# Staggering the first batch of an attention and FFN kernel: loads, weight conversion, norms and evictions moved between steps, and denominators by products with ones

## The chip, the core and the metric

The kernel runs on one core of one Trainium2 chip. The metric is the device time of one execution in microseconds (us); below it is the median of the runs shown. Profiles are of one execution each, taken by the hardware profiler. TensorE is written PE (its weight loads PEld), VectorE DVE, ScalarE ACT, GpSimd POOL, SyncE SP.

## What is computed

Attention over 8 batches, 12 heads, 448 positions, head dimension 64, with RMS norms of q and k, and then an FFN with a squared ReLU on 3584 tokens:

```
q_n, k_n = rmsnorm(q, g_q), rmsnorm(k, g_k)      # x / sqrt(mean(x*x) + 1e-6) * g
scores = matmul(q_n, k_n.T) / sqrt(64)
attn = exp(scores - max)
attn = attn / (sum(attn) + 1e-09)
x = matmul(attn, v)                              # (B,H,S,D) -> (B*S, H*D) = (3584, 768)
h = maximum(x @ w_in, 0.0)                       # w_in 768 x 2048
out = (h * h) @ w_out                            # w_out 2048 x 768
```

q, k, v are float32. The two weights reach the kernel as 64-bit floats, so it turns them into float32 itself.

## The kernel before

A flag computed from the gains chooses between two programs; the runs here take the one without the shift by the maximum (`shift=False`). Its work goes by pairs of heads: six pairs per batch, 48 in all (0 to 47), and four steps (`n` = 0 to 3) per pair, one for each quarter of the keys. Within a step the instructions are written out in an order that the engines keep (`manual_schedule`): every engine, and SP's DMA queue, works through its own instructions in program order and waits at each for what it needs.

For pair `i`:

- `load_qk` (L112) and `load_v` (L126) are DMAs on SP, into two buffers each.
- `normalize` (L135): per q and k, ACT squares, DVE reduces (L142), both times through the one buffer `squares`; DVE scales (L143), POOL raises to the power -1/2 (`rr`, L147; 112 x 16 numbers) and multiplies q by it (`qn`, L152). k's factor goes into the exponential's scale.
- `turn` (L165): eight transposes on PE into banks 2 and 3 (L173), DVE evicts qT with the gain (L175), ACT evicts kT (L179).
- `weigh` (L186), step `m`: PE's scores of both heads (L195) into banks 0 and 1 or, in odd steps, 2 and 3; ACT's exponentials (L197); `add_up` (L202) sums the weights of the steps, one head on POOL, one on DVE (L211).
- `attend` (L236), one pair later: PE multiplies weights and v (L244), accumulating over the four steps; in step 1 the summed weights are multiplied by ones (L251), which gives the denominators on the right partitions; DVE takes the reciprocal (L261), and after step 3 the product `xT` (L265).

A step of pair `i` issues `weigh(i, n)` and `attend(i - 1, n)`; step 0 also `normalize(i + 1)`, step 2 `turn(i + 1)`, step 3 `load_v(i + 1)`.

The FFN of batch b runs as a stream of pieces during batch b + 1, from its second pair on, so that the first pair of each batch has no FFN beside it. `ffn` (L279) first makes the 16 hidden tiles (L287, ACT's ReLU L296, squares on POOL L301 to L306) through banks 6 and 7, then the output tiles (L316), and stores them.

The weights stay in SBUF. They come in 56 chunks, 24 of w_in (128 x 512) and 32 of w_out (128 x 384). One chunk's conversion (`to_float32`, L365) is three ACT operations (L374 to L376) on the high and low words, a clamp on POOL (L377), and three DVE operations that join them (L382, L386, L390). The raw words of w_in lie in eight buffers (shared with `h2`), those of w_out in two (shared with `y`). `load_weights` (L352) issues a chunk's DMA and its conversion together, at the beginning of a step: one chunk per step in batch 0, three per step from pair 6 on.

The lines that the change and the prediction speak of are in these functions:

Of the kernel before, what the change touches and what calls it, by code (L numbers as in the profile page):

```python
# [10 lines left out]
F32 = mybir.dt.float32  # L11
# [22 lines left out]
def kernel(  # L34
# [33 lines left out]
    with tc.If(flag > 0) as either:  # L68
        program(tc, q, k, v, g_q, g_k, moe_w_in, moe_w_out, out, shift=False)
    with either.Else():  # L70
        program(tc, q, k, v, g_q, g_k, moe_w_in, moe_w_out, out, shift=True)
# [3 lines left out]
def program(ctx, tc, q, k, v, g_q, g_k, moe_w_in, moe_w_out, out, shift):  # L75
# [21 lines left out]
    gg = const.tile([P, 2], F32, name="gg")  # L97
# [12 lines left out]
    loaded, values, normal, turned, weights, sums, dens, xts = {}, {}, {}, {}, {}, {}, {}, {}  # L110
# [23 lines left out]

    def normalize(i):  # L135
# [10 lines left out]
        rr = small.tile([CP, 2, 2 * NJ], F32, name="rr", tag="rr", bufs=3)  # L146
# [89 lines left out]
    def attend(i, m):  # L236

        b, c = pairs[i]
        vt = values[i]
        if m == 0 and c == 0:  # L240
            xts[b] = [None] * NC
        av = banks[4 + i % 2][:, 0:S]
        for e in range(2):
            nc.tensor.matmul(  # L244
                av[ds(e * D, D), :], lhsT=vt[:, e, m, :], rhs=weights.pop((i, e, m)),
                start=m == 0, stop=m == NJ - 1,
            )
        if m == 1:
            den = banks[5 - i % 2][:, 0:S]
            for e in range(2):  # L250
# [12 lines left out]
        if m == NJ - 1:  # L263
            xT = ffn_p.tile([P, S], F32, name="xT", tag="xT", bufs=NC + 2)
            nc.vector.tensor_tensor(out=xT, in0=av, in1=dens.pop(i), op=ALU.mult)  # L265
            xts[b][c] = xT
            del turned[i], normal[i], values[i]
# [74 lines left out]
    def weight_chunks():  # L342
# [5 lines left out]
        for f in range(NF):  # L348
            for half in range(2):
                yield w_out_sb[:, f, ts(half, HALF)], moe_w_out[ts(f, P), :], half * HALF  # L350

    def load_weights(dst, rows, col):  # L352
        n = dst.shape[1]
        if rows.dtype == F32:
# [4 lines left out]
        words = ffn_p.tile([P, n, 2], U32, name="words", tag=tag, bufs=bufs)  # L359
        nc.sync.dma_start(  # L360
            words.rearrange("p n w -> p (n w)"), rows.bitcast(U32)[:, 2 * col : 2 * (col + n)]
        )
        to_float32(dst, words[:, :, 0], words[:, :, 1])

    def to_float32(dst, low, high):  # L365
# [15 lines left out]
        bits = dst.bitcast(U32)  # L381
# [9 lines left out]

    load_qk(0)
    for e in range(2):
        for n, gain in enumerate((g_q, g_k)):
            nc.scalar.dma_start(gg[ds(e * D, D), n : n + 1], gain.rearrange("(d one) -> d one", one=1))
    nc.vector.scalar_tensor_tensor(
        out=g, in0=gg[:, 0:1], scalar=D**-0.5, in1=gg[:, 1:2], op0=ALU.mult, op1=ALU.mult
    )
    nc.vector.memset(minus_half, -0.5)
    nc.vector.memset(ones, 1.0)  # L400
    make_identity(nc, ident)
    load_qk(1)
    load_v(0)
# [4 lines left out]
    chunks = deque(weight_chunks())  # L408

    with tc.manual_schedule(engines=ENGINES):  # L410
        normalize(0)
        turn(0)
        stream, pieces, done = iter(()), 0, 0
        for i, (b, c) in enumerate(pairs):
            if i + 2 < len(pairs):
                load_qk(i + 2)
            for n in range(NJ):
                step = c * NJ + n
                if step == NJ and b:
                    stream, pieces, done = ffn(b - 1), ffn_pieces(b - 1), 0  # L420
                for _ in range(1 if b == 0 else len(chunks) if shift else 3):
                    if chunks:
                        load_weights(*chunks.popleft())
# [3 lines left out]
                if shift and n == 0 and i:  # L427
                    for m in range(NJ):
                        attend(i - 1, m)
                weigh(i, n)  # L430
                if i and not shift:
                    attend(i - 1, n)
                if n == 0 and i + 1 < len(pairs):
                    normalize(i + 1)
                if n == 2 and i + 1 < len(pairs):
                    turn(i + 1)
                if n == NJ - 1 and i + 1 < len(pairs):
                    load_v(i + 1)
            if c == NPAIR - 1:
                for _ in stream:  # L440
                    pass
        for n in range(NJ):
            attend(len(pairs) - 1, n)
# [32 lines left out]
```

## Time and profile before

| | us |
|---|---|
| median of 3 runs (1873.43 to 1875.64) | 1874.79 |
| the profiled execution, its own time | 1875.46 |
| its span in the trace | 1873.4 |
| PE busy (share of the span) | 1675.4 (89%) |
| PE weight loads | 784.3 (42%) |
| DVE, ACT, POOL busy | 533.8, 473.6, 551.7 |
| mean granted clock of PE | 0.934 |

Busy time is the time an engine had an instruction in work; a matmul of float32 shows as several records (passes). The granted clock is given as a share of 2.4 GHz: 1.00, or 0.50 for 1.2 GHz, and values between are means over both. Times in rows are us from the start of the span; a bracket at the end of a row tells how long the engine sat idle before it, and what it waited for last.

### The profile page before, as it was taken

How to read it: one execution, taken by the hardware profiler on the slowest of the kernel's cores; microseconds unless marked ns; L12 is line 12 of the kernel's file. 1: busy time of each engine (PE TensorE's matmuls, PEld its weight loads, DVE VectorE, ACT ScalarE, POOL GpSimd, SP SyncE). 2: the span in 40 equal slices, each digit the busy share in tenths (PEclk: the TensorE clock that was granted, in tenths of full speed). 3: DMA queues.
4: the chain of work that ended last, by engine and by line, in shares of the span. 5: the costliest groups of instructions: out<-in, count | busy, mean ns of one | idle time of the engine just before them, and what ended most of it. 6: DMA issues, size and time to landing. Idle time of an engine off the chain costs nothing.

```text
span 1873.4 us, 14405 instructions
## 1 busy us (share of the span) xinstructions
PE 1675.4 (89%) x5440; PEld 784.3 (42%) x5440; DVE 533.8 (28%) x634; ACT 473.6 (25%) x853; POOL 551.7 (29%) x558
## 2 busy tenths in 40 slices
PE   3454367999999999999999999999999999999998
PEld 1111123454445544454445544454445534454555
DVE  3555555323212132223122222223222232212000
ACT  3435355312221122212221122212221132211100
POOL 3424233422332124313332224313341133311200
PEclk7665579999999999999999999999999999999999
DMA  4132243011010110011100110011000110000000
GB/s 139 60 105 74 82 116 108 23 32 38 22 24 24 32 38 15 16 38 32 30 15 24 32 38 15 20 42 38 15 15 24 32 38 15 20 22 9 0 9 27
DMA packets 80531, 70.24 MB, mean 37 GB/s; under 512 B 48196, under 2 KB 69700, under 8 KB 80452
## 3 DMA queue, kind: packets, MB, share of 16 engines
q1 hardware_dynamic: 80128, 69.23, 13.2%
q8 instruction: 45, 0.74, 0.2%
q14 instruction: 34, 0.28, 0.1%
q10 hardware_dynamic: 324, 0.00, 0.0%
HBM read 58.20 MB, written 11.01 MB: 37 GB/s over the span
## 4 chain that ended last, share of the span: by engine, by line
PE 80%; issue 5%; DVE 4%; POOL 4%; DMA 3%; ACT 2%; SPq 1%; POOLq 0%; ACTq 0%; DVEq 0%
PE bank L316 31%; PE bank L287 30%; PE bank L195 8%; PE bank L244 7%; POOL rr L147 2%; DMA words<-in_moe_w_out_dram 2%; PE bank L173 2%; PE bank L251 1%; DMA words<-in_moe_w_in_dram 1%; DVE rden L261 1%; POOL words L377 1%; DVE sum L211 1%; ACT words L374 1%; DVE w_in_sb L386 1%; DVE w_in_sb L382 1%
## 5 line engine op out<-in xcount | busy, mean ns | idle before, releaser
L287 PE MATMUL bank<-xT,w_in_sb 128*128 128x448 f32 x1536 | 612.1, 554 | 22.0 <-ACT h L296 20.7
L316 PE MATMUL bank<-w_out_sb,h 128*128 128x384 f32 x1792 | 593.9, 489 | 0.0
L316 PEld LDWEIGHTS bank<-w_out_sb,h 128*128 128x128 f32 x1792 | 335.5, 190 | 253.9 <-issue 32.2
L287 PEld LDWEIGHTS bank<-xT,w_in_sb 128*128 128x128 f32 x1536 | 291.4, 194 | 335.3 <-issue 287.6
L197 ACT ACTIVATE wT<-bank,rr 112x448 f32<-112x448 f32 x384 | 221.9, 629 | 553.9 <-PE bank L195 549.4
L195 PE MATMUL bank<-qT,kT 64*112 64x448 f32 x768 | 219.3, 638 | 101.2 <-DVE qT L175 70.6
L211 POOL TENSOR_TENSOR sum<-sum,wT 112x448 f32<-112x448 f32 x96 | 111.9, 1165 | 410.8 <-ACT wT L197 410.0
L211 DVE TENSOR_TENSOR sum<-sum,wT 112x448 f32<-112x448 f32 x96 | 109.8, 1143 | 421.3 <-ACT wT L197 421.3
L147 POOL TENSOR_TENSOR rr<-ms,minus_half 112x16 f32<-112x16 f32 x48 | 139.5, 2905 | 302.8 <-DVE ms L143 302.8
L244 PE MATMUL bank<-wT,vt 112*64 112x448 f32 x768 | 200.8, 605 | 0.0
L296 ACT ACTIVATE h<-bank 128x448 f32<-128x448 f32 x128 | 69.2, 542 | 424.1 <-PE bank L287 424.1
L195 PEld LDWEIGHTS bank<-qT,kT 64*112 64x112 f32 x768 | 61.8, 186 | 223.1 <-issue 101.4
L142 DVE TENSOR_REDUCE ms<-squares 112x8 f32<-112x512 f32 x96 | 65.8, 686 | 298.1 <-ACT squares L141 297.6
L261 DVE RECIPROCAL rden<-bank 128x448 f32<-128x448 f32 x48 | 141.5, 2948 | 1.2 <-PE bank L251 1.2
L306 POOL TENSOR_TENSOR h<-h 128x448 f32<-128x448 f32 x64 | 59.7, 932 | 183.3 <-ACT h L296 183.3
L211 DVE TENSOR_TENSOR sum<-wT 112x448 f32<-112x448 f32 x48 | 35.2, 734 | 228.6 <-PE bank L251 227.5
L244 PEld LDWEIGHTS bank<-wT,vt 112*64 112x64 f32 x768 | 40.4, 142 | 140.7 <-issue 140.7
L301 POOL TENSOR_TENSOR h<-h 128x384 f32<-128x384 f32 x64 | 53.3, 832 | 147.0 <-ACT h L296 147.0
L211 POOL TENSOR_TENSOR sum<-wT 112x448 f32<-112x448 f32 x48 | 71.0, 1479 | 75.9 <-PE bank L251 74.9
L173 PE MATMUL bank<-ident,qn 112*128 112x112 f32 x192 | 32.5, 298 | 67.8 <-POOL qn L152 51.3
L323 DVE COPY y<-bank 128x384 f32<-128x384 f32 x28 | 15.3, 548 | 229.8 <-PE bank L316 229.8
L141 ACT ACTIVATE squares<-qk 112x512 f32<-112x512 f32 x96 | 60.3, 628 | 39.8 <-DVE ms L142 39.7
(36 smaller groups left out, 580.7 us busy)
## 6 DMA issues: line engine op xcount, KB each, us to landing
words<-in_moe_w_in_dram SPq DMA_DIRECT2D x24, 512.0 KB, 6.6
words<-in_moe_w_out_dram SPq DMA_DIRECT2D x32, 384.0 KB, 3.1
qk<-in_q_dram SPq DMA_DIRECT2D x48, 224.0 KB, 3.3
qk<-in_k_dram SPq DMA_DIRECT2D x96, 112.0 KB, 3.5
vt<-in_v_dram SPq DMA_DIRECT2D x48, 224.0 KB, 2.9
out_dram<-y SPq DMA_DIRECT2D x8, 336.0 KB, 2.8
out_dram<-y SPq DMA_DIRECT2D x8, 288.0 KB, 2.7
out_dram<-y SPq DMA_DIRECT2D x8, 240.0 KB, 2.6
```

Source lines behind the costliest of these rows:

```text
L141: nc.scalar.activation(squares, qk[:, x], AF.Square)
L142: nc.vector.tensor_reduce(out=ms[:, ts(x, 2 * NJ)], in_=squares, axis=AX.X, op=ALU.add)
L147: nc.gpsimd.tensor_tensor(out=rr.rearrange("p x r -> p (x r)"), in0=ms, in1=minus_half.to_broadcast([CP, 4 * NJ]), op=ALU.pow,)
L173: nc.tensor.transpose(tr[:, ts(j, CP)], rows[:, j].rearrange("p h d -> p (h d)"), ident[:CP, :CP])
L195: nc.tensor.matmul(sc, lhsT=kT[r, ts(m, CP)], rhs=qT[r, :], start=True, stop=True)
L197: nc.scalar.activation(weights[i, e, m], sc, AF.Exp, scale=normal[i][2][:, 2 * m + e : 2 * m + e + 1])
L211: engine.tensor_tensor(out=sums[i, e], in0=so_far, in1=weights[i, e, m], op=ALU.add)
L244: nc.tensor.matmul(av[ds(e * D, D), :], lhsT=vt[:, e, m, :], rhs=weights.pop((i, e, m)), start=m == 0, stop=m == NJ - 1,)
L261: nc.vector.reciprocal(out=rden, in_=den)
L287: nc.tensor.matmul(ps, lhsT=w_in_sb[:, c, ts(f, P)], rhs=xT[c], start=c == 0, stop=c == NC - 1,)
L296: nc.scalar.activation(h[:, at : at + S], ps, AF.Relu)
L316: nc.tensor.matmul(ps, lhsT=h2[f][:, ts(n, P)], rhs=w_out_sb[:, f, ts(half, HALF)], start=f == 0, stop=f == NF - 1,)
```

## The change

Conversion of a chunk is cut in three and spread over steps: `load_weights(k)` issues only the DMA, `split_words(k)` the ACT and POOL part, `join_words(k)` the DVE part, one chunk behind. They are called at the end of a step, and w_in's chunks are loaded three ahead. For w_in, the last of ACT's three operations goes to POOL. w_out's chunks come by halves of the columns. One chunk per step is now taken through pair 6, three per step after it.

The squares of pair i + 2 are taken in step 3 of pair i, into two buffers. The eviction `xT` becomes `finish`, called in step 0 of the next pair but one. `load_v(i)` and `load_qk(i + 2)` stand behind it in step 0 of pair i.

In batch 0 (`alone`), the weights aren't summed: each step's weights are multiplied by ones, accumulating over four steps in bank 6 or 7, and the reciprocal follows step 3. The gain column `g` comes from a small matmul on the row that the flag was computed from; its own four DMAs go.

```diff
-    loaded, values, normal, turned, weights, sums, dens, xts = {}, {}, {}, {}, {}, {}, {}, {}
+    loaded, values, squared, normal, turned, weights, sums, dens, xts = {}, {}, {}, {}, {}, {}, {}, {}, {}
...
+    def square(i):
+        squares = [
+            att.tile([CP, 2 * NJ, D], F32, name="squares", tag="squares") for _ in range(2)
+        ]
+        for x in range(2):
+            nc.scalar.activation(squares[x], loaded[i][:, x], AF.Square)
+        squared[i] = squares
+
     def normalize(i):
...
-        for x in range(2):
-            squares = att.tile([CP, 2 * NJ, D], F32, name="squares", tag="squares", bufs=1)
-            nc.scalar.activation(squares, qk[:, x], AF.Square)
+        for x, squares in enumerate(squared.pop(i)):
             nc.vector.tensor_reduce(out=ms[:, ts(x, 2 * NJ)], in_=squares, axis=AX.X, op=ALU.add)
...
     def add_up(i, m):
 
-        if m == 0:
+        if m == 0 or pairs[i][0] == 0:
             return
...
     def attend(i, m):
...
+        alone = b == 0
         av = banks[4 + i % 2][:, 0:S]
+        den = banks[6 + i % 2 if alone else 5 - i % 2][:, 0:S]
...
+        for e in range(2):
+            wT = weights.pop((i, e, m))
+            if alone:
+                nc.tensor.matmul(
+                    den[ds(e * D, D), :], lhsT=ones, rhs=wT, start=m == 0, stop=m == NJ - 1
+                )
+            elif m == 1:
                 nc.tensor.matmul(
                     den[ds(e * D, D), :], lhsT=ones, rhs=sums.pop((i, e)), start=True, stop=True
                 )
+        if m == (NJ - 1 if alone else 1):
...
-        if m == NJ - 1:
-            xT = ffn_p.tile([P, S], F32, name="xT", tag="xT", bufs=NC + 2)
-            nc.vector.tensor_tensor(out=xT, in0=av, in1=dens.pop(i), op=ALU.mult)
...
+    def finish(i):
...
+        xT = ffn_p.tile([P, S], F32, name="xT", tag="xT", bufs=NC + 2)
+        nc.vector.tensor_tensor(
+            out=xT, in0=banks[4 + i % 2][:, 0:S], in1=dens.pop(i), op=ALU.mult
+        )
...
+    def split_words(k):
...
         nc.scalar.activation(high.bitcast(F32), high.bitcast(F32), AF.Copy, scale=REBIAS)
-        nc.scalar.activation(low.bitcast(F32), low, AF.Copy, scale=2.0**-29, bias=2.0**23)
-        nc.scalar.activation(low, low.bitcast(F32), AF.Copy, bias=-(2.0**23))
         nc.gpsimd.tensor_scalar(
             out=high.bitcast(F32), in0=high.bitcast(F32), scalar1=MOST, scalar2=-MOST,
             op0=ALU.min, op1=ALU.max,
         )
+        nc.scalar.activation(low.bitcast(F32), low, AF.Copy, scale=2.0**-29, bias=2.0**23)
+        if k < 4 * NC:
+            nc.gpsimd.tensor_scalar(
+                out=low, in0=low.bitcast(F32), scalar1=-(2.0**23), scalar2=1.0,
+                op0=ALU.add, op1=ALU.mult,
+            )
+        else:
+            nc.scalar.activation(low, low.bitcast(F32), AF.Copy, bias=-(2.0**23))
...
+    def convert(k):
+
+        join_words(k - 1)
+        if k + 3 < 4 * NC:
+            load_weights(k + 3)
+        elif k + 1 >= 4 * NC:
+            load_weights(k + 1)
+        split_words(k)
+
     load_qk(0)
+    load_weights(0)
+    load_qk(1)
+    load_weights(1)
+    load_weights(2)
...
         for i, (b, c) in enumerate(pairs):
...
             for n in range(NJ):
                 step = c * NJ + n
+                if n == 0:
+                    if i > 1 and not shift:
+                        finish(i - 2)
+                    load_v(i)
+                    if i + 2 <= last:
+                        load_qk(i + 2)
...
-                for _ in range(1 if b == 0 else len(chunks) if shift else 3):
-                    if chunks:
-                        load_weights(*chunks.popleft())
...
+                if i < last:
+                    if n == 0:
+                        normalize(i + 1)
+                    if n == 2:
+                        turn(i + 1)
+                    if n == NJ - 1 and i + 2 <= last:
+                        square(i + 2)
+                for _ in range(1 if i < NPAIR + 1 else 3):
+                    if piece <= len(chunks):
+                        convert(piece)
+                        piece += 1
```

## Rows read from the trace of the kernel before

**Rows 1.** The span in 40 slices, granted clock of PE in tenths

```profile
PEclk7665579999999999999999999999999999999999
```

**Rows 2.** Windows: from:to, length, busy time per engine (instructions), PE clock, DMA share, GB/s

```profile
97.30:128.80 31.50, 15.13 (x46) 4.66 (x46) 17.22 (x22) 13.12 (x23) 10.82 (x9) 0.61 0.27 89
...
193.10:245.50 52.40, 18.42 (x52) 5.57 (x52) 27.46 (x44) 22.31 (x44) 13.08 (x16) 0.57 0.34 99
...
245.50:338.00 92.50, 70.53 (x205) 30.44 (x204) 52.73 (x82) 48.17 (x95) 40.65 (x51) 0.88 0.36 103
338.00:456.90 118.90, 118.90 (x402) 57.64 (x401) 28.45 (x32) 24.41 (x44) 29.75 (x28) 1.00 0.09 25
```

**Rows 3.** The chain that ended last, one round in batch 0: start, us, what

```profile
81.80 2.90 POOL rr L147
...
91.39 2.87 DVE rden L261
...
97.28 1.84 PE bank L195 x4
...
103.07 4.35 DMA words<-in_moe_w_in_dram
```

**Rows 4.** Instructions by time, first pair of batch 3: start, us, engine, line

```profile
681.04 0.69 DVE L142 TENSOR_REDUCE ms<-squares 112x8 f32<-112x512 f32 x1 [0.69 <-ACT squares L141]
...
682.01 2.90 POOL L147 TENSOR_TENSOR rr<-ms,minus_half 112x16 f32<-112x16 f32 x1 [4.13 <-DVE ms L143]
...
686.09 0.60 PE L173 MATMUL bank<-ident,qn 112*128 112x112 f32 x4 [2.97 <-POOL qn L152]
...
687.47 2.06 PE L195 MATMUL bank<-qT,kT 64*112 64x448 f32 x4 [0.40 <-DVE qT L175]
```

**Rows 5.** Groups by line, 66 to 193 us: count, busy us, mean ns

```profile
L152 POOL TENSOR_TENSOR qn<-qk,rr 112x512 f32<-112x512 f32 x4 | 4.2, 1042 | 0.3
...
L265 DVE TENSOR_TENSOR xT<-bank,rden 128x448 f32<-128x448 f32 x4 | 2.4, 610 | 0.0
```

**Rows 6.** Instructions by time, one round of batch 0

```profile
99.05 1.76 PE L244 MATMUL bank<-wT,vt 112*64 112x448 f32 x4
...
104.88 0.97 PE L244 MATMUL bank<-wT,vt 112*64 112x448 f32 x4
...
108.18 0.64 POOL L377 TENSOR_SCALAR words<-words 128x512 f32<-128x512 f32 x1 [7.12 <-ACT words L374]
...
108.85 0.43 DVE L382 TENSOR_SCALAR w_in_sb<-words 128x512 uint32<-128x512 uint32 x1 [6.77 <-POOL words L377]
...
109.31 0.69 DVE L386 SCALAR_TENSOR_TENSOR w_in_sb<-words,w_in_sb 128x512 uint32<-128x512 uint32 x1
...
110.14 0.69 DVE L390 CUSTOM_DVE_ANT_0 w_in_sb<-words,w_in_sb 128x1024 uint16<-128x1024 uint16 x1
...
117.98 1.35 DVE L382 TENSOR_SCALAR w_in_sb<-words 128x512 uint32<-128x512 uint32 x1 [4.77 <-POOL words L377]
...
119.37 1.01 DVE L386 SCALAR_TENSOR_TENSOR w_in_sb<-words,w_in_sb 128x512 uint32<-128x512 uint32 x1
...
120.51 1.41 DVE L390 CUSTOM_DVE_ANT_0 w_in_sb<-words,w_in_sb 128x1024 uint16<-128x1024 uint16 x1
```

**Rows 7.** Instructions by time, the start

```profile
16.70 0.68 DVE L175 TENSOR_SCALAR qT<-bank,g 128x448 f32<-128x448 f32 x1 [5.28 <-PE bank L173]
```

**Rows 8.** Instructions by time, chunks of w_out and PE beside them

```profile
205.94 6.41 SPq L360 DMA_DIRECT2D words<-in_moe_w_out_dram  x3
...
209.13 0.54 ACT L374 ACTIVATE words<-words 128x384 f32<-128x384 f32 x1 [3.24 <-DMA words<-in_moe_w_out_dram]
...
211.40 0.56 DVE L390 CUSTOM_DVE_ANT_0 w_out_sb<-words,w_out_sb 128x768 uint16<-128x768 uint16 x1
...
275.74 9.69 PE L287 MATMUL bank<-xT,w_in_sb 128*128 128x448 f32 x18 [8.28 <-ACT h L296]
...
298.91 4.78 PE L287 MATMUL bank<-xT,w_in_sb 128*128 128x448 f32 x12 [2.10 <-ACT h L296]
```

**Rows 9.** Window: the first pair of batch 3, from the wait on (columns as in rows 2)

```profile
682.00:698.00 16.00, 12.64 (x37) 5.37 (x36) 6.85 (x6) 3.44 (x7) 7.68 (x5) 0.79 0.19 43
```

More of the change, by code (lines that the diff above doesn't have):

```diff
@@ L1 @@
-from collections import deque
 from contextlib import ExitStack
@@ L145, in normalize @@
         )
-        rr = small.tile([CP, 2, 2 * NJ], F32, name="rr", tag="rr", bufs=3)
+        rr = small.tile([CP, 2, 2 * NJ], F32, name="rr", tag="rr", bufs=4)
         nc.gpsimd.tensor_tensor(
@@ L347, in weight_chunks, with load_weights @@
                 yield w_in_sb[:, c, ts(blk, n)], moe_w_in[ts(c, P), :], blk * n
-        for f in range(NF):
-            for half in range(2):
+        for half in range(2):
+            for f in range(NF):
                 yield w_out_sb[:, f, ts(half, HALF)], moe_w_out[ts(f, P), :], half * HALF
-    def load_weights(dst, rows, col):
+    chunks = list(weight_chunks())
+    words = {}
+    def load_weights(k):
+        if k >= len(chunks):
+            return
+        dst, rows, col = chunks[k]
         n = dst.shape[1]
@@ L380, in to_float32, with join_words @@
         )
-        bits = dst.bitcast(U32)
+        nc.scalar.activation(low.bitcast(F32), low, AF.Copy, scale=2.0**-29, bias=2.0**23)
[6 more added lines that the diff above has]
+            nc.scalar.activation(low, low.bitcast(F32), AF.Copy, bias=-(2.0**23))
+    def join_words(k):
+        if k not in words:
+            return
+        both = words.pop(k)
+        low, high = both[:, :, 0], both[:, :, 1]
+        bits = chunks[k][0].bitcast(U32)
         nc.vector.tensor_scalar(
@@ L390, in to_float32 @@
         nc.vector.tensor_tensor(out=bits, in0=bits, in1=low, op=ALU.add)
-    load_qk(0)
-    for e in range(2):
[L394 to L400, printed above, removed]
+    def convert(k):
[5 more added lines that the diff above has]
+        split_words(k)
+    load_qk(0)
+    load_weights(0)
+    load_qk(1)
+    load_weights(1)
+    load_weights(2)
+    nc.vector.memset(ones, 1.0)
+    nc.vector.memset(minus_half, -0.5)
+    gains = banks[0][:, 0:1]
+    for e in range(2):
+        nc.tensor.matmul(gains[ds(e * D, D), :], lhsT=g_row, rhs=ones[0:1, 0:1], start=True, stop=True)
+    nc.vector.tensor_scalar(out=g, in0=gains, scalar1=D**-0.5, scalar2=None, op0=ALU.mult)
     make_identity(nc, ident)
-    load_qk(1)
-    load_v(0)
     steps = NPAIR * NJ
-    chunks = deque(weight_chunks())
+    last = len(pairs) - 1
     with tc.manual_schedule(engines=ENGINES):
+        square(0)
         normalize(0)
         turn(0)
-        stream, pieces, done = iter(()), 0, 0
+        square(1)
+        stream, pieces, done, piece = iter(()), 0, 0, 0
         for i, (b, c) in enumerate(pairs):
-            if i + 2 < len(pairs):
-                load_qk(i + 2)
             for n in range(NJ):
                 step = c * NJ + n
+                if n == 0:
[4 more added lines that the diff above has]
+                        load_qk(i + 2)
                 if step == NJ and b:
                     stream, pieces, done = ffn(b - 1), ffn_pieces(b - 1), 0
-                for _ in range(1 if b == 0 else len(chunks) if shift else 3):
-                    if chunks:
-                        load_weights(*chunks.popleft())
+                    while shift and piece <= len(chunks):
+                        convert(piece)
+                        piece += 1
                 while shift and step == NJ and done < pieces or done * (steps - NJ) < pieces * (step - NJ + 1):
@@ L429, in program @@
                         attend(i - 1, m)
+                    finish(i - 1)
                 weigh(i, n)
@@ L432, in program @@
                     attend(i - 1, n)
[L433 to L438, printed above, removed]
+                if i < last:
[7 more added lines that the diff above has]
+                    if piece <= len(chunks):
+                        convert(piece)
+                        piece += 1
             if c == NPAIR - 1:
@@ L441, in program @@
                     pass
+        if not shift:
+            finish(last - 1)
         for n in range(NJ):
-            attend(len(pairs) - 1, n)
+            attend(last, n)
+        finish(last)
         for _ in ffn(B - 1):
```

30 lines of the change are left out of this document (14 added, 16 removed).

## The prediction

> **What bounds the kernel now.** I read the slices first, then windows of stages, then the chain of waits in the first batch, then single instructions. In the slices [rows 1] the granted clock is low up to about 340 us and full after: the loss sits in the first fifth of the span. The windows [rows 2] say the same in busy time. One pair of heads of batch 0 takes 31.5 us, and no engine is full in it: PE 15.1, DVE 17.2, ACT 13.1, POOL 10.8 us. From 338.0 to 456.9 PE is busy 118.9 of 118.9 us for 13 steps, so a dense step costs 9.15 us. The seven steps before (245.5 to 338.0) took 92.5 us, 28.5 more than dense. The pair before those took 52.4 us.
>
> The chain [rows 3] shows why a pair takes 31.5 us: it goes round through one DMA of a weight chunk (4.35 us, queued behind q, k and v), ACT's conversion, POOL's power (2.90), DVE's conversion, DVE's reciprocal (2.87), PE, and back to the DMA. Work that belongs to one pair waits for weights that the attention doesn't need. In the trace by time [rows 4] DVE's reduce waits for ACT's squares, and ACT for the reduce: they alternate on one buffer.
>
> **The change, part by part: batch 0.** Chunks now arrive three steps early, conversion stands last in a step, squares are taken in the last step of the pair before, and DVE joins a chunk one step late. Chunk transfers leave the path: four chunks, q, k and v must pass in a pair of some 21 us, where they pass in 31.5 today with the DMA engines at 0.27 [rows 2]. SP's order still puts v and q, k of later pairs ahead of a chunk; v waits for the attend of two pairs back, which is over when the pair begins, so a chunk is late by a step at most, with three to spare.
>
> What remains is a ring through queues that keep program order. With the reduces of the next pair as its start:
> - two reduces (0.69 each) and the scaling (0.17 and some 0.25 to POOL): 1.8. Here squares are ready, so nothing alternates [rows 4].
> - the power 2.90 [rows 3], then qn 1.04 [rows 5] and hand-over: 4.05, so 5.85.
> - POOL's two operations of the chunk behind them. The clamp is 0.64 [rows 6]. The second (add, times one, float to unsigned) is new on POOL, and no row shows it. Its ends are nothing, since it may overlap, and 2.9 us, POOL's longest operation [rows 3]. I take 0.64, as shape and kind are the clamp's; both 1.4, so 7.25.
> - DVE's join of that chunk. Alone its three instructions run from 108.85 to 110.83, 1.98 us; beside a busy POOL from 117.98 to 121.92, 3.94 us [rows 6]. POOL is busy with the next chunks then, with single-input work only; I take the middle, 2.9, so 10.15.
> - qT stands behind the join on DVE: 0.68 [rows 7] and 0.1, so 10.95. PE's last scores of the pair need the bank and wait for it.
> - PE has then been idle over 4 us and is at 1.2 GHz: scores 1.84 [rows 3], attend 1.76 [rows 6], product with ones 0.9 to 1.76, taken as 1.3 since the clock comes back meanwhile. Together 4.9, so 15.85.
> - the reciprocal 2.9, a join alone 1.9, finish 0.61 [rows 5], hand-over 0.1: 21.3 us, when the next reduces start.
>
> So 21.3 us a pair instead of 31.5. Ends: 18.2 if PE keeps 2.4 GHz (attend 0.97, [rows 6], the other two as much: minus 2.0) and the join runs alone (minus 1); 24.7 if both joins run at the contended price (plus 1 and 2) and the last product at half clock. A pair of batch 0 has four groups of products with ones instead of one; three lie where PE waits, the last is in the ring. Sums leave DVE and POOL in batch 0; the ring is written without them. ACT gives one of three conversion operations to POOL; ACT, 13.1 busy of 31.5 [rows 2], is in no term.
>
> The start: qT of pair 0 ends at 17.38 [rows 7], and the new gain (a matmul of one row with ones, one small scaling) needs only data that are there before q lands. That and the new loads behind q and k of pair 0 count nothing; uncovered, 1 us. Pair 0 has nothing to attend: 21.3 minus 8.5 (PE, reciprocal, finish) plus one join more in series, 14.7. Pairs 1 to 5 take five rings, 106.5. Pair 6 runs until PE ends pair 5: the ring up to there, with narrower chunks, one POOL operation less and its own sums on DVE, 15.4. The FFN starts at 17.4 + 14.7 + 106.5 + 15.4 = 154.0 instead of 245.5 [rows 2]: **minus 91.5 us.**
>
> **The steps with FFN and conversion.** Before, 20 chunks remain at 245.5; after, 28. They use two buffers, a load only one ahead. Today's cycle [rows 8]: the load begins at 205.94, ACT starts at 209.13 and the join ends at 211.96, so 6.0 us for two buffers, 3.0 a chunk, 9.0 a step of three chunks: as much as a dense step of 9.15. So each hold-up shows on PE. The large ones are the 8.28 us [rows 8] and one like it a pair later: power and qn hold the clamp, the clamp the join, the join the next load, and ACT, waiting for that load, holds the FFN's ReLU. The change keeps this mechanism and now passes three normalizations in the stretch, not two, each shorter by the alternation of squares. I take 7 us for each with the clock it costs, and 5 for the rest: 183 dense plus 26, 209, against 92.5 + 118.9 = 211.4: **minus 2.** Ends: 195 (three times 4 only) and 223 (1.4 us per chunk as today). The order of w_out's chunks and finish one step later hide: the first output tile comes after step 11, the chunks end in step 9.
>
> **The first pair of each later batch.** No FFN covers it, and today transposes wait 2.97 us for qn [rows 4], six times in the trace. With squares a step earlier the alternation goes (the second reduce ended at 681.73; it would end near 680.4): transposes 1.3 us earlier, 8 us in six batches. Their 1.26 us on ACT now delay the first exponentials by some 0.5, which nobody awaits there. The wait left is about 1.7 us. After 2.97 us the clock falls to 1.2 GHz each time: it averages 0.79 in 16 us [rows 9], 3.4 us lost, in one of the six 5.1. After a wait of 2.10 us PE kept 2.4 GHz, 12 passes in 4.78 us [rows 8]. So I expect the fall to go: 19 of the 22 us. **Minus 27.** Elsewhere FFN matmuls cover the moved squares; uncovered, some 1 us a pair.
>
> **Sum.** The profiled execution took 1875.46 us, 2.1 beyond its span and 0.7 above the median. 1875.5 − 91.5 − 2 − 27 = 1755.0, which I give as 1755.
>
> **The rivals.**
> - *The clock still falls in the six pairs.* A wait of 1.7, transposes, and 0.3 for qT make 3.0 us without other products. Against it stands the 2.10 us wait. For it: in [rows 4] transposes ran at full clock and the scores right behind them lost it, so they had not kept it up. Then 19 us stay: 1774. The Trainium skill, TensorE: Matmul & The Clock Gate, Part 4 (PE-mode transpose), says that transposes don't count as PE being busy; by that rule this is the case to expect, and the trace, with one fall after transposes, agrees without settling it. 0.25.
> - *Batch 0 stays slower:* both joins contended (24.7 a pair, plus 17) and 1.4 us per chunk later (plus 14): 1786. For it: every POOL and DVE instruction shared time at 118 [rows 6]. 0.13.
> - *PE keeps its clock in batch 0* (18.2 a pair, minus 15.5) and normalizations cost only themselves (minus 14): 1725. Against: waits of over 4 us in the ring. 0.08.
> - *It doesn't do what it says:* SP's waits keep chunks late, pairs stay at 31.5: 5 times 10.2, 1806. Against: three chunks in hand. 0.02.
> - *Slower than before:* POOL's new conversion to unsigned is slow. POOL then sets the pair: 3.95 + 4 × (0.64 + x). To eat 120 us over six pairs that must be 41.3, so x is 8.7 us or more. For it: POOL needs 2.90 us for 16 columns of a power [rows 3], so its price can be far from its size. Against: three times that for plain arithmetic. 0.02.
>
> **How the numbers follow.** The forecast has 0.50. Its own ends (18.2 to 24.7 a pair, 195 to 223) give some 1728 to 1785; the range reaches to the fallen clock with a slower batch 0 and to most of the fast case: 1724 to 1798, leaving out under 2 in 10. A measurement of this kernel tells about 0.2% from no change; only the last rival is not faster by that: faster 0.97, same 0.01, slower 0.02.
>
> **What would show it.** Right: power operations of batch 0 about 21 us apart; first FFN matmul near 154; POOL's new operation near 0.65; DVE's qT directly behind a join with PE waiting for it; transposes waiting 1.7 us at the later batches' starts and clock 1.00 there. Wrong: a DMA ahead of ACT's conversion in batch 0, FFN steps far above 9.15 us up to the last chunk, or 0.8 of the clock in the six first pairs.

## The result, and the profile after

The changed kernel takes 1766.75 us (median of 4 runs, 1761.29 to 1768.19), the kernel before 1875.22 on the same chip (4 runs): a ratio of 0.942, 95% interval 0.939 to 0.944. The forecast was 1755, range 1724 to 1798. The profiled execution of after took 1766.63 us.

First the page of after: its span, and the granted clock in 40 slices, which answers to [rows 1]. The first six slices read 7 to 9 where they read 5 to 7.

```profile
span 1764.8 us, 14547 instructions
...
PEclk8878989999999999999999999999999999999999
```

Three windows of after (columns as in [rows 2]): one pair of batch 0; the first 99 us of the FFN; from there to batch 2's first scores.

```profile
109.30:129.28 19.98, 14.71 (x58) 5.06 (x56) 13.46 (x19) 10.49 (x20) 10.67 (x10) 0.74 0.19 56
145.25:244.50 99.25, 80.84 (x232) 34.98 (x231) 53.12 (x85) 48.67 (x98) 40.94 (x53) 0.91 0.36 98
244.50:361.57 117.07, 112.72 (x377) 54.79 (x375) 40.29 (x54) 33.32 (x64) 35.41 (x34) 0.97 0.17 49
```

A pair fell from 31.5 to 19.98 us, with PE busy about as long (15.1 before, 14.7 now). Cut at the first FFN matmul and at batch 2's first scores:

| stage, us | before | after | change | predicted |
|---|---|---|---|---|
| start to FFN | 245.5 | 145.25 | −100.3 | −91.5 |
| FFN to batch 2's first scores | 211.4 | 216.3 | +4.9 | −2 |
| from there to the end | 1416.5 | 1403.2 | −13.3 | −27 |
| span | 1873.4 | 1764.8 | −108.6 | −120.5 |

The round in batch 0, instructions of after by time:

```profile
109.32 1.27 DVE L146 TENSOR_REDUCE ms<-squares 112x8 f32<-112x512 f32 x2
...
110.88 3.01 POOL L151 TENSOR_TENSOR rr<-ms,minus_half 112x16 f32<-112x16 f32 x1 [5.80 <-DVE ms L147]
...
115.07 1.01 PE L177 MATMUL bank<-ident,qn 112*128 112x112 f32 x4 [3.13 <-POOL qn L156]
115.10 0.66 POOL L403 TENSOR_SCALAR words<-words 128x512 f32<-128x512 f32 x1
115.79 0.43 DVE L422 TENSOR_SCALAR w_in_sb<-words 128x512 uint32<-128x512 uint32 x1 [3.11 <-POOL words L403]
115.84 0.90 POOL L409 TENSOR_SCALAR words<-words 128x512 uint32<-128x512 f32 x1
...
118.25 0.67 DVE L179 TENSOR_SCALAR qT<-bank,g 128x448 f32<-128x448 f32 x1
...
118.97 1.84 PE L199 MATMUL bank<-qT,kT 64*112 64x448 f32 x4 [2.15 <-DVE qT L179]
...
120.74 1.76 PE L252 MATMUL bank<-wT,vt 112*64 112x448 f32 x4
...
122.28 1.71 PE L259 MATMUL bank<-wT,ones 112*64 112x448 f32 x4
...
124.04 2.96 DVE L274 RECIPROCAL rden<-bank 128x448 f32<-128x448 f32 x1 [2.70 <-PE bank L259]
...
128.75 0.61 DVE L283 TENSOR_TENSOR xT<-bank,rden 128x448 f32<-128x448 f32 x1
129.28 0.67 DVE L146 TENSOR_REDUCE ms<-squares 112x8 f32<-112x512 f32 x1
```

This is the predicted ring, link by link, and no DMA stands in it. PE waits twice, 3.13 us for the normalization and 2.15 for qT, which stands on DVE behind a chunk's join.

In the FFN stage PE waits for ACT's ReLU (PE's instructions by time, the rows with the longest of these waits):

```profile
181.22 4.78 PE L307 MATMUL bank<-xT,w_in_sb 128*128 128x448 f32 x12 [2.67 <-ACT h L316]
...
192.95 6.47 PE L307 MATMUL bank<-xT,w_in_sb 128*128 128x448 f32 x12 [5.11 <-ACT h L316]
...
218.30 7.46 PE L307 MATMUL bank<-xT,w_in_sb 128*128 128x448 f32 x12 [5.04 <-ACT h L316]
...
231.58 9.90 PE L307 MATMUL bank<-xT,w_in_sb 128*128 128x448 f32 x18 [3.06 <-ACT h L316]
...
256.24 4.10 PE L307 MATMUL bank<-xT,w_in_sb 128*128 128x448 f32 x5 [4.12 <-ACT h L316]
```

ACT in turn waits for the transfers of w_out's chunks, and SP issues these late, since it waits for the DVE joins that free their two buffers (waits in this stage: us in all, times, longest):

```profile
ACT words L402 <- DMA words<-in_moe_w_out_dram: 54.9, 20, 7.4
SPq L386 <- DVE w_out_sb L430: 104.1, 28, 10.1
```

Before, ACT waited there 37.5 us in 13 times.

The first pair of batch 2, by time (answers to [rows 4]), and three of the six windows of 16 us from there on (answer to [rows 9]):

```profile
369.31 0.60 PE L177 MATMUL bank<-ident,qn 112*128 112x112 f32 x4 [1.40 <-POOL qn L156]
369.62 1.20 DVE L215 TENSOR_TENSOR sum<-sum,wT 112x448 f32<-112x448 f32 x1
...
370.75 0.67 DVE L179 TENSOR_SCALAR qT<-bank,g 128x448 f32<-128x448 f32 x1
371.48 1.84 PE L199 MATMUL bank<-qT,kT 64*112 64x448 f32 x4 [1.18 <-DVE qT L179]
```

```profile
365.57:381.57 16.00, 13.42 (x43) 5.36 (x40) 8.29 (x9) 4.47 (x9) 7.25 (x6) 0.79 0.17 48
583.50:599.50 16.00, 13.48 (x46) 5.50 (x46) 8.24 (x9) 4.43 (x8) 8.44 (x8) 0.89 0.17 45
779.10:795.10 16.00, 13.43 (x49) 6.16 (x48) 8.30 (x9) 4.43 (x8) 7.87 (x7) 1.00 0.16 45
```

Transposes now wait 1.40 us instead of 2.97, but the scores behind them 1.18 instead of 0.40: the sum went from 3.37 to 2.58 us. The clock still fell in five of the six windows (0.79, 0.89, 1.00, 0.79, 0.89, 0.79).

### The profile page after: what moved, and what is told of

Same layout as the page of the kernel before. It is cut to its first block, busy times and chain, and to the rows that moved or that the text cites. A ratio compares the mean times of both kernels' runs of the same rounds, so it can differ in the third digit from the quotient of the medians.

```text
span 1764.8 us, 14547 instructions
## 1 busy us (share of the span) xinstructions
PE 1670.1 (95%) x5516; PEld 781.7 (44%) x5516; DVE 503.3 (29%) x616; ACT 453.9 (26%) x829; POOL 553.6 (31%) x564
## 3 DMA queue, kind: packets, MB, share of 16 engines
q1 hardware_dynamic: 80128, 69.23, 13.7%
## 4 chain that ended last, share of the span: by engine, by line
PE 83%; issue 5%; DVE 4%; POOL 3%; ACT 2%; DMA 2%; POOLq 0%; ACTq 0%; DVEq 0%; SPq 0%
PE bank L336 33%; PE bank L307 30%; PE bank L199 9%; PE bank L252 8%; DMA words<-in_moe_w_out_dram 2%; POOL rr L151 2%; PE bank L263 2%; PE bank L177 2%; DVE sum L215 1%; POOL words L403 1%; ACT wT L201 1%; DVE w_out_sb L426 1%; DVE qT L179 1%; ACT words L402 0%; DVE w_out_sb L422 0%
## 5 line engine op out<-in xcount | busy, mean ns | idle before, releaser
L307 PE MATMUL bank<-xT,w_in_sb 128*128 128x448 f32 x1536 | 611.8, 554 | 22.8 <-ACT h L316 20.9
L199 PE MATMUL bank<-qT,kT 64*112 64x448 f32 x768 | 206.1, 616 | 25.9 <-DVE qT L179 25.3
L215 DVE TENSOR_TENSOR sum<-sum,wT 112x448 f32<-112x448 f32 x84 | 98.5, 1173 | 412.9 <-ACT wT L201 412.9
L215 POOL TENSOR_TENSOR sum<-sum,wT 112x448 f32<-112x448 f32 x84 | 98.8, 1176 | 359.6 <-ACT wT L201 358.5
L252 PE MATMUL bank<-wT,vt 112*64 112x448 f32 x768 | 194.6, 588 | 0.0
L215 DVE TENSOR_TENSOR sum<-wT 112x448 f32<-112x448 f32 x42 | 26.5, 632 | 483.1 <-PE bank L263 468.1
L274 DVE RECIPROCAL rden<-bank 128x448 f32<-128x448 f32 x48 | 141.6, 2951 | 13.7 <-PE bank L259 12.5
L215 POOL TENSOR_TENSOR sum<-wT 112x448 f32<-112x448 f32 x42 | 64.0, 1524 | 202.1 <-PE bank L263 202.1
L199 PEld LDWEIGHTS bank<-qT,kT 64*112 64x112 f32 x768 | 56.3, 181 | 143.8 <-issue 95.8
L343 DVE COPY y<-bank 128x384 f32<-128x384 f32 x28 | 15.4, 549 | 257.8 <-PE bank L336 257.8
L345 ACT COPY y<-bank 128x384 f32<-128x384 f32 x28 | 13.4, 479 | 216.8 <-PE bank L336 204.2
L177 PE MATMUL bank<-ident,qn 112*128 112x112 f32 x192 | 30.9, 287 | 34.6 <-POOL qn L156 34.6
L403 POOL TENSOR_SCALAR words<-words 128x384 f32<-128x384 f32 (+1 forms) x56 | 37.0, 662 | 81.6 <-ACT words L402 80.1
```

The lines of the kernel that those rows point to most:

```text
L177: nc.tensor.transpose(tr[:, ts(j, CP)], rows[:, j].rearrange("p h d -> p (h d)"), ident[:CP, :CP])
L199: nc.tensor.matmul(sc, lhsT=kT[r, ts(m, CP)], rhs=qT[r, :], start=True, stop=True)
L252: nc.tensor.matmul(av[ds(e * D, D), :], lhsT=vt[:, e, m, :], rhs=weights[i, e, m], start=m == 0, stop=m == NJ - 1,)
L274: nc.vector.reciprocal(out=rden, in_=den)
L307: nc.tensor.matmul(ps, lhsT=w_in_sb[:, c, ts(f, P)], rhs=xT[c], start=c == 0, stop=c == NC - 1,)
L403: nc.gpsimd.tensor_scalar(out=high.bitcast(F32), in0=high.bitcast(F32), scalar1=MOST, scalar2=-MOST, op0=ALU.min, op1=ALU.max,)
```

## The experiments

Every run has its edit against after. Single executions of after vary by 7 us, with the mean granted clock (0.972 in the shortest, 0.965 in the longest), so single runs are read by their stages. In the four versions that leave batch 0 as in after (after, e7, e8, e10) the FFN starts between 144.1 and 145.3, so a change of 1 us there says nothing. "Round" is the mean distance of POOL's powers from the second to the eighth (six distances), read from POOL's instructions by time.

| run | to FFN | FFN to batch 2 | rest | span | round |
|---|---|---|---|---|---|
| before | 245.5 | 211.4 | 1416.5 | 1873.4 | 30.9 |
| after | 145.25 | 216.3 | 1403.2 | 1764.8 | 18.8 |
| e1_sums | 141.84 | 213.1 | 1395.9 | 1750.8 | 18.5 |
| e2_squares_late | 148.96 | 223.8 | 1397.3 | 1770.1 | 19.0 |
| e3_low_on_act | 140.79 | 216.3 | 1400.4 | 1757.5 | 18.2 |
| e4_zero_ahead | 144.61 | 217.3 | 1402.2 | 1764.1 | 18.7 |
| e5_conv_first | 146.49 | 222.1 | 1404.9 | 1773.5 | 18.8 |
| e6_first_zero | 154.96 | 220.2 | 1400.5 | 1775.6 | 19.4 |
| e11_join_now | 188.22 | 219.9 | 1403.2 | 1811.3 | 24.4 |
| e9_qt_first | 135.37 | 215.7 | 1402.0 | 1753.1 | 17.1 |
| e10_norm_last | 144.27 | 214.7 | 1402.1 | 1761.1 | 18.7 |
| e8_turn_matmul | 144.11 | 216.5 | 1394.1 | 1754.7 | 18.7 |
| e7_fill | 145.34 | 216.8 | 1380.7 | 1742.9 | 18.8 |
| e12_best | 143.85 | 214.5 | 1380.7 | 1739.1 | 18.8 |

The first distance has no pair to attend, so the round of after (18.8) is a mean of 14.1 and five of some 19.8.

**Batch 0: which part carries the 100 us?** Each part was first undone alone.

*Denominators by sums in batch 0 again:*

```diff
-        if m == 0 or pairs[i][0] == 0:
+        if m == 0:
...
-        alone = b == 0
+        alone = False
```

> Denominators of batch 0 by sums again, all else as in the changed kernel. Theory (the ring of batch 0 is what its queues' order makes of it): the reciprocal (2.9 us) and the last product with ones leave the end of the ring, since the reciprocal follows step 1; in exchange DVE takes two sums of 0.6 to 1.2 us inside the ring and POOL three of 1.14 beside it, which lengthens the joins. So the powers of batch 0 stand 19 to 20.5 us apart, as now (19.9), and the total stays within 6 us of 1766. Rival (the products with ones are what frees the ring): POOL's 3.4 us of sums lie in it, powers 23 to 24 us apart, total 20 to 25 us more.

FFN start 3.4 us earlier, rounds of 18.5. The reciprocal then runs in step 1, while DVE would otherwise wait for POOL; by products with ones it comes at the end of the round and three groups of products lie on PE's path. This part of the change costs a little. The total, 14 us less, lies outside both expectations; 7.3 us of it come behind batch 2's first scores, where the clock fell in two places of six.

*Squares in the same step as the reduces again:*

```diff
-                    if n == NJ - 1 and i + 2 <= last:
-                        square(i + 2)
...
                     if n == 0:
+                        square(i + 1)
                         normalize(i + 1)
```

> Squares taken in step 0 right before the reduces again, though into two buffers. Theory: in batch 0 the squares stand behind one pair of exponentials on ACT, 0.8 us a ring or 5 us in all; in the first pair of each later batch the wait of the transposes grows from 1.40 to about 1.9 us and the clock falls six times of six: 3 to 11 us. Total 1774 to 1782. Rival (early squares matter nowhere): total within 3 us of 1766.

FFN start 3.7 us later, 3.0 of them before the second power; the mean round stayed within 0.2 us. The FFN stage lost 7.5 us; PE waited 25.7 us there for the ReLU, where it waits 20.9 in after, and why stays open. In the later batches the expectation was wrong: the waits turned round, 2.2 us for qn and 0.4 for qT, and the clock fell in one of six windows, not in six.

*ACT's third operation back on ACT:*

```diff
-        if k < 4 * NC:
+        if k < 0:
             nc.gpsimd.tensor_scalar(
```

> The last of the three operations on a w_in chunk goes back from POOL to ACT. Theory: in the trace DVE's join starts when the clamp ends, not when this operation ends, and is slowed by POOL beside it; without it the ring loses the slowing alone, some 0.5 us, so powers 19.2 to 19.6 us apart and a total 2 to 5 us lower. Rival (POOL's time is in the ring): minus 0.75 and more a pair, 18.9 or less. Rival (ACT becomes the bound with 0.67 more per chunk): powers further apart than 20.5.

FFN start 4.5 us earlier, 3.4 of them in the first two rounds; the other four together are as in after (78.4 us against 78.8). The total, 7 us less, is more than the 2 to 5 expected. POOL's operation L409 took 0.65 us alone and up to 0.98 beside DVE; it buys nothing.

*Chunks loaded in their own step, and conversion at the start of a step, each alone:*

```diff
-        if k + 3 < 4 * NC:
-            load_weights(k + 3)
-        elif k + 1 >= 4 * NC:
+        if k < 4 * NC:
+            load_weights(k)
+        if k + 1 >= 4 * NC:
             load_weights(k + 1)
...
-    load_weights(0)
     load_qk(1)
-    load_weights(1)
-    load_weights(2)
```

> w_in's chunks are loaded in the step that converts them, not three steps ahead; conversion stays last in the step. Theory: PE is done with a pair some 5 us before the next ring begins, SP then issues v, q, k and the chunk, and the chunk is needed by POOL only behind power and qn, 6 us after the ring's begin; so its 5 us transfer is covered and powers stay 19.9 to 21 us apart, total 0 to 7 us more. Rival (loading ahead is what takes the transfer off the path): powers go back towards 31 us apart, total 40 to 70 us more.

> Conversion back at the beginning of a step, ahead of its scores; loads stay three ahead. Theory: POOL now works a chunk ahead of the power and one less between qn and the join that holds qT, but DVE gets one join more into the ring; powers of batch 0 19.5 to 21.5 us apart, total within 8 us of 1766. Rival (the place of the conversion carries the gain, since the exponentials stand behind it): powers 25 us apart or more, total 30 us more or worse.

(In the second the loop that calls `convert` is moved, unchanged, from the end of a step to its start.) FFN start −0.6 and +1.2 us: neither alone matters in batch 0. (The second costs 5.8 us in the FFN stage.) *Both together:*

> Both at once: conversion at the beginning of a step and each w_in chunk loaded in that step. Theory (either place takes the transfer off the path, only both together put it on): ACT waits in step 0 for v, q, k and the chunk, some 7 us after PE's end, the exponentials and the power stand behind it: powers 22 to 26 us apart, total 15 to 40 us more, and more than the two single edits added. Rival (they add): the sum of the two single edits' losses.

+9.7 us at the FFN's start, 6 of them before the second power, with later rounds of 19.0 to 20.9 us, where the theory had 22 to 26. More than the two alone, but a tenth of the gain: with the rest of the change in place, a chunk's transfer in the chain costs little. What was left unlike before is, among other things, DVE's order. There a chunk's join stood in the chunk's own step, so DVE sat at it until POOL had clamped, with qT and the reciprocal behind it. So the next run undoes that too:

```diff
         split_words(k)
+        if k < 4 * NC:
+            join_words(k)
```

> Edit: the run with the transfer issued only in its own step and the conversion at the step's start (FFN start 154.96 us, powers 20.5 us apart, span 1775.6) plus one thing more, in batch 0 a chunk's three DVE joins stand in its own step again instead of one step later; early squares and denominators by products with ones stay. Theory (DVE's queue held by a join that waits for POOL's clamp, with the next pair's qT and the reciprocal behind it, is what made a pair of batch 0 cost 29 us before): powers 26 to 31 us apart, FFN start at 200 to 235 us, span 1820 to 1860. Rival (the early squares and the products with ones carry the gain, wherever the join stands): powers at most 22 us apart, FFN start at most 170 us, span at most 1792.

FFN start 188.22, 33 us later than without this edit. Four of the six distances are 26.2 to 26.7 us, at the lower end of the theory's; the first and the last are 20.0 and 20.7, and so the FFN start lies 12 us and the span 9 us under its range. Instructions of one round of this run by time:

```profile
120.89 0.65 ACT L402 ACTIVATE words<-words 128x512 f32<-128x512 f32 x1 [6.60 <-DMA words<-in_moe_w_in_dram]
...
122.30 0.43 DVE L422 TENSOR_SCALAR w_in_sb<-words 128x512 uint32<-128x512 uint32 x1 [4.23 <-POOL words L403]
...
126.08 2.91 POOL L151 TENSOR_TENSOR rr<-ms,minus_half 112x16 f32<-112x16 f32 x1 [2.85 <-DVE ms L147]
...
130.88 0.43 DVE L422 TENSOR_SCALAR w_in_sb<-words 128x512 uint32<-128x512 uint32 x1 [4.88 <-POOL words L403]
...
133.32 0.86 DVE L422 TENSOR_SCALAR w_in_sb<-words 128x512 uint32<-128x512 uint32 x1
...
136.18 0.67 DVE L179 TENSOR_SCALAR qT<-bank,g 128x448 f32<-128x448 f32 x1
```

DVE sits at a join for 4.23 and 4.88 us. From the second of these to qT two joins stand, not one: 5.30 us (130.88 to 136.18), where after has 2.46. The first stands ahead of the reduces, and POOL's power waits 2.85 us for them. But the clamp that this first join waits for comes late because ACT sat 6.60 us at the chunk's transfer. So the edit brings back some 5 us of a round's fall (24.4 against 19.4), the largest part found, but measured only with the transfer back in its step; a join in its own step with the loads three ahead was not run.

The other 57 of the 100 us, from this FFN start (188.2) to that of before (245.5), stay without an experiment. They hold the early squares, the products with ones, `finish` and `load_v` moved, one ACT operation fewer, and one chunk per step, not three, in pair 6; the early squares, the products and the ACT operation, undone alone, cost at most 4 us each, the rest was not undone. Where they lie can be told: from the seventh power (in pair 5) to the FFN start before takes 67.9 us, this run 35.4, after 34.4. So 32 of the 57 lie at the end of the stretch, where before converts three chunks per step. That points to the number of chunks in pair 6, which no run put back.

*The join that stands ahead of qT moved behind it, in batch 0:*

```diff
-        join_words(k - 1)
+        if not late:
+            join_words(k - 1)
...
+                        if i < NPAIR and n == 2:
+                            join_words(piece - 2)
-                        convert(piece)
+                        convert(piece, late=i < NPAIR and n == 1)
```

> In batch 0 the join of step 1 is put behind the transposes' eviction in step 2, so that qT on DVE no longer stands behind a join. Theory (qT behind the join is the place where PE waits in the ring): PE's wait for qT of 2.15 us goes, powers 17 to 18.2 us apart, total 9 to 15 us less. Rival (DVE's work is the bound in any order): powers stay at 19.5 to 20 us, the wait moves to the reciprocal.

FFN start 9.9 us earlier, powers 17.4 to 17.7 us apart from the third power on, as the theory said. The two rows to look at are qT directly behind the transposes, and PE's wait for it, 0.47 instead of 2.15 us:

```profile
90.05 0.60 PE L177 MATMUL bank<-ident,qn 112*128 112x112 f32 x4 [3.74 <-POOL qn L156]
...
90.76 0.69 DVE L179 TENSOR_SCALAR qT<-bank,g 128x448 f32<-128x448 f32 x1 [3.10 <-PE bank L177]
91.36 0.42 DVE L422 TENSOR_SCALAR w_in_sb<-words 128x512 uint32<-128x512 uint32 x1
...
91.50 1.98 PE L199 MATMUL bank<-qT,kT 64*112 64x448 f32 x4 [0.47 <-DVE qT L179]
```

**The FFN stage.** *From pair 7 on, the normalization issued behind a step's conversions:*

```diff
-                    if n == 0:
+                    if n == 0 and i <= NPAIR:
                         normalize(i + 1)
...
+                if n == 0 and NPAIR < i < last:
+                    normalize(i + 1)
```

> From pair 7 on the norm of step 0 comes behind that step's three conversions, so that POOL's clamps don't stand behind power and qn. Theory (in the steps with FFN and conversion the chain of two buffers sets the time and each norm holds it by the 3.95 us of power and qn): three norms, 8 to 14 us less from the first FFN product to the next batch's first scores (now 216.3 us). Rival (ACT's wait for DMAs alone holds the ReLU): no change within 4 us; later norms could then hold transposes and cost some us.

1.6 us less in this stage; PE waits 16.8 us for the ReLU instead of 20.9. So the power and qn ahead of the clamp, the mechanism that I gave for this stage's hold-ups, are not what most of them wait for. What remains is ACT at the next chunk's DMA (45.2 us here, 54.9 in after), with the ReLU behind it; no run took that wait away (more buffers for w_out's words might), so its share stays argued.

**The first pair of each later batch.** *A batch's first transposes as products with the identity:*

```diff
-                nc.tensor.transpose(tr[:, ts(j, CP)], rows[:, j].rearrange("p h d -> p (h d)"), ident[:CP, :CP])
+                part = rows[:, j].rearrange("p h d -> p (h d)")
+                if pairs[i][1] == 1:
+                    nc.tensor.matmul(
+                        tr[:, ts(j, CP)], lhsT=part, rhs=ident[:CP, :CP], start=True, stop=True
+                    )
+                else:
+                    nc.tensor.transpose(tr[:, ts(j, CP)], part, ident[:CP, :CP])
```

> The transposes that belong to the first pair of a batch (eight in the program) are done as products with the identity instead of in the transpose mode. The waits before and behind them stay. Cost on PE some 0.5 to 0.7 us each, 5 us in all. Theory A (what PE does in transposes doesn't keep the clock up, products do): the clock stays at 1.00 in four or more of the six places, mean granted clock of the runs above 0.975, total 0 to 10 us less. Theory B (the waits alone let it fall): falls in five or six of six as now, mean clock 0.965 to 0.970, total 3 to 8 us more.

1756.63 us (4 runs, 1756.32 to 1757.02), ratio to before 0.936 (0.935 to 0.938). The wait ahead is the same, the clock is 1.00 in all six windows:

```profile
368.30 1.15 PE L179 MATMUL bank<-ident,qn 112*128 112x112 f32 x8 [1.39 <-POOL qn L156]
...
369.28 1.06 PE L179 MATMUL bank<-ident,qk 112*128 112x112 f32 x8
...
370.46 1.50 PE L205 MATMUL bank<-qT,kT 64*112 64x448 f32 x4
```

With transposes the waits of PE (place, us in all, times, longest) from batch 2 on are these in after and, to a tenth, in eight of its variants (e1, e3 to e6, e9 to e11):

```profile
PE bank L177 <- POOL qn L156: 8.2, 6, 1.4
PE bank L199 <- DVE qT L179: 7.1, 6, 1.2
```

In these nine the clock fell in 41 of 54 such windows. The products also take twice as long (8 passes), so they fill the wait for qT: this run can't part "transposes don't keep the clock up" from "the second wait is shorter". The run with late squares speaks for the second wait: transposes there too, one fall in six, with these waits:

```profile
PE bank L177 <- POOL qn L156: 13.2, 6, 2.2
PE bank L199 <- DVE qT L179: 2.0, 5, 0.4
```

Before, with 2.97 and 0.40, it fell six times.

*Two FFN pieces of a batch held back, one each ahead of that first pair's transposes and its next scores:*

```diff
+                if c == 0 and n == NJ - 1:
+                    for _ in stream:
+                        pass
                 weigh(i, n)
...
                     if n == 2:
+                        if c == 0:
+                            next(stream, None)
                         turn(i + 1)
```

(`held = 2` pieces are taken out of the even spreading over a batch's steps, and what is left of the stream runs at the end of the next batch's first pair.)

> The last two pieces of each FFN (8 passes each, 2.65 us) are kept for the next batch's first pair: one ahead of its transposes, one ahead of its last scores, where PE waits 1.40 and 1.18 us now. Theory (these waits cost their length and let the clock fall): both waits vanish, the clock stays at 1.00 in the six places; 15.5 us of waits and the 13.7 us that the clock costs now, so 25 to 30 us less, 1737 to 1742. Rival (the clock falls for another reason, such as the transposes themselves): 12 to 16 us less, clock still below 1 there. Rival (the held work only pushes others back): within 5 us.

1742.83 us (4 runs, 1741.45 to 1744.73), ratio to before 0.929 (0.927 to 0.930): 24 us under after. It is just over the expected time. From batch 2 on PE's waits are gone but for 0.7 us, and with transposes as in after the clock is 1.00 in all six windows. The place in question, PE by time, and the first of these windows:

```profile
367.54 0.97 PE L252 MATMUL bank<-wT,vt 112*64 112x448 f32 x4
368.44 2.85 PE L336 MATMUL bank<-w_out_sb,h 128*128 128x384 f32 x8
371.13 0.55 PE L177 MATMUL bank<-ident,qn 112*128 112x112 f32 x4
```

```profile
367.39:383.39 16.00, 16.00 (x57) 7.99 (x56) 7.80 (x9) 4.91 (x9) 7.11 (x7) 1.00 0.25 68
```

So transposes alone don't bring the clock down; waits beside them are needed. The last stage fell by 22.5 us. Waits of 2.58 us in six batches are 15.5 of them; by the other 7.1 PE was busy less. Yet PE had more to do there: two pieces (16 of w_out's passes, 5.2 us) now lie behind batch 2's first scores, and the stage that they left got no shorter (216.8 against 216.3). So the clock gave some 12 us, an estimate from these numbers, near the 13.7 expected, and the two pieces are most of what is missing.

**Held pieces, qT first and sums together:**

> Three edits together: two FFN pieces held back for the next batch's first pair (alone 1742.8 us), in batch 0 the join of a pair's second step behind qT (alone -9.9 us at the FFN's start), denominators of batch 0 by sums again (alone -3.4 us at the FFN's start). Theory (both batch 0 edits shorten the same round on DVE and PE at different places and mostly add; the held pieces act in other batches): powers of batch 0 16 to 17 us apart, FFN start at 131 to 135 us, 1725 to 1733 us. Rival (with the join behind qT the round hangs on ACT's conversion, so the sums give nothing more, or their DVE additions take the place of the join): powers 17.5 us or more apart, FFN start at 135 to 140 us, 1733 to 1740 us.

1740.50 us (4 runs, 1739.02 to 1740.97), ratio to before 0.928 (0.926 to 0.929), the lowest time of all versions, but only 2.3 us under the held pieces alone, which the two intervals don't part. The FFN start, 143.85, lies outside both expectations; the rounds are the rival's. The batch 0 edits don't add: where they gave 9.9 and 3.4 us alone, together they give 1.5. The window of one round of this run shows why:

```profile
93.21:111.99 18.78, 13.39 (x46) 3.50 (x44) 18.06 (x22) 10.48 (x19) 15.49 (x13) 0.77 0.31 99
```

DVE is busy 18.06 of 18.78 us. With the sums (and POOL's sums beside them, where the operations of both take longer) DVE itself is the bound, and an order of its queue can give little. Held pieces with qT first and products with ones, by the stages an estimated 10 us under 1742.8, was not run.

## Why the prediction was right, and where it was not

The sign, the size and the place were right: 1766.6 against 1755, as three errors of −8.8, +6.9 and +13.7 us. That the total is so near is partly luck, since the first of them covers more than half of the last.

**Batch 0, the ring: right, a little long.** Predicted 21.3 us a round, measured 19.1 to 20.0. By its terms, from the rows of after: reduces and scaling 1.56 (1.8); power, qn and hand-over 4.2 (4.05); POOL ahead of the join 0.7 (1.4), because the join starts behind the clamp and the second operation runs beside it; the join 2.46 (2.9); qT 0.72 (0.78); scores, attend and ones at half clock 5.07 (4.9); reciprocal, join and finish 5.24 (5.5). Together 19.95. The terms that were too long are the second POOL operation, which is not in series, and the contended join. The new POOL operation cost 0.65, as taken; the "slower" rival needed 8.7. What I did not see is that the products with ones cost more than the sums would (rounds of some 19.8 against 18.5): I counted them at the end of the ring and took the sums out, but the reciprocal they push back had lain in DVE's wait.

The start and pair 0 took 16.4 and 14.1 us (17.4, 14.7), the last pair to the FFN 16.0 (15.4). So the rivals with a slow batch 0, with chunks that stay late, and with PE at full clock there are out.

**The reason I gave for the old round was at best half of it.** I read the chain [rows 3] as a loop through a chunk's DMA; the forecast didn't rest on that, since the new ring was added up by itself. With the DMA back in its step and the conversion first, the FFN start moved by 9.7 us of the 100; with the join back in its step too, by another 33. In both runs the chain that ended last goes through that DMA again, with 4 to 5 us of it in a round. So, as these two runs read, the transfer costs much only where a join stands between it and the next power; the remaining 57 us stay open. The chain did show "DVE's conversion, DVE's reciprocal"; that DVE stood idle at joins in [rows 6] (6.77 and 4.77 us for POOL's clamp), the second time with the reciprocal and qT behind it, was in rows that I had used only for durations.

**The FFN stage: +4.9 instead of −2.** Loss over the dense steps 33.3 us where I took 26, inside my ends. The step that failed is its mechanism, "power and qn hold the clamp": issued last, they gave back 1.6 us. ACT's wait for the transfers, 54.9 us in this stage, is the larger one.

**The later batches: −13.3 instead of −27.** The step that failed is "so I expect the fall to go". The rival at 0.25 happened in five of six pairs. In this stage PE's idle time fell by 4.2 us, where I took 8, and its busy time, by the clock, by 9.1, where I took 19. The wait for qn is 1.40, under the 1.7 that I took, but the wait for qT is 1.18, where I took 0.3: with the power earlier, DVE has just begun the sum, 1.20 us beside POOL's own sum, when the bank is ready, and qT stands behind it. It is the same fault as in batch 0, a small instruction behind a long one on DVE, and I had costed qT at the wait of the old order. The Trainium skill, TensorE: Matmul & The Clock Gate, Part 4 (PE-mode transpose), says that transpose mode doesn't count as PE being busy in the same way. By that the clock should fall with transposes and stay with products; 41 of 54 against none of 6 agrees with it, with the reserve above, but the one fall in six with late squares, transposes too, doesn't follow from it alone.

## What to carry to other kernels

On an engine that keeps program order, an instruction that waits for another engine holds whatever stands behind it (here qT, for which PE waited some 2.1 us a round): put the consumer a step later than the producer, and put small instructions that PE waits for ahead of long ones. Undo parts one by one before crediting any: here three of the parts (products with ones, the operation moved to POOL, loads ahead), undone singly, cost no time or even saved some, and two edits that each gained gave almost nothing together, since they filled DVE. And undo the plain part too: the number of chunks in pair 6, which I did not undo, may hold a third of the gain. A stretch without filler work is worth more than its waits: two FFN pieces held for it gave 24 us, where the waits were 15.5, with one edit in the schedule and none in the arithmetic.

## What the runs showed of the hardware that I had not expected

- With equal waits, 1.4 us ahead of eight transposes and 1.2 behind, the clock fell in some batches and stayed in others of one execution (five of six in after, two of six with the sums). With 2.2 us ahead and 0.4 behind it fell once in six, though the sums of the waits are alike; with the waits filled and the transposes kept it never fell. What decides between the first two stays open.
- Two reduces in a row took 1.27 us together, where one alone takes 0.69.
- DVE's L426 took 0.69 us alone and 1.02 beside POOL, POOL's L409 0.65 and 0.98. Whether both run slower or take turns inside these times the rows don't tell: beside each other (116.7 to 118.9 us in after) their operations end in turn, 0.5 to 0.6 us apart.
